# Scores behind the down projection, the last p*v ahead of it, and three edits that go with them, in a fused attention and gated-FFN kernel

## The chip, the core and the metric

One NeuronCore of a Trainium2 chip runs the whole program. Its engines are TensorE (PE: matmuls; PEld: the loads of their stationary operands), VectorE (DVE), ScalarE (ACT), GpSimd (POOL) and SyncE (SP, which here issues every DMA). The metric is the device time of one execution in microseconds, lower is better. Times in the text are microseconds unless marked otherwise.

## The reference

x has 2048 rows of D = 576. One branch is sliding-window attention with 32 heads of 18, the other a gated FFN of width 4608, and the two are multiplied.

```python
xn = _layernorm(x)
qkv = (xn @ wqkv) -> q, k, v, 32 heads of 18
scores = einsum("bhqd,bhkd->bhqk", q, k) * 18 ** -0.5
mask = (0 <= i - j) & (i - j < 256)
s = (softmax(where(mask, scores, -1e9)) @ v) @ wo
h = sigmoid(xn @ w_gate) * (xn @ w_up)
return x + s * silu(h @ w_down)
```

## The kernel before

**Chunks.** The rows are worked in four chunks of 512 (`NCH`, `CH`), each in four blocks of 128. A chunk has these stages on TensorE:

- *Projections* (L485): twelve passes, q, k and v of four blocks. For chunks 1 to 3 they stand between the down blocks 1 and 2 of the chunk before (`QKV_F2`). VectorE and ScalarE copy q and k out of PSUM, and transposing DMAs bring them into `qkp`.
- *Gate/up* (L873): 36 tiles of 128 columns of F, each with nine contraction steps. Two matmuls run at a time, one on rows 0 to 63 of the array (the low stream) and one on rows 64 to 127 (the high stream); a pair is called a step here. A tile's gate and up each take one of the banks 6, 7, 5, 4. ScalarE reads gate with a tanh (L887), VectorE combines it with up (L891) into `hT`. Since each stream does one of the two matrices, one gate tile, number `XS[c]`, has two of its steps moved to the high stream, ahead of its own turn, with weights loaded for it apart (`load_x`, L833); from there on gate ends two steps ahead of up.
- *Attention* between the gate/up steps: a score visit (L631) takes all of the banks 0 to 3 and feeds two exponentials on ScalarE (L649); VectorE applies the mask (L667). Chunks 1 to 3 have twenty such visits, chunk 0 sixteen. After each pair of head groups comes a p*v visit (L701), four in a chunk, also in banks 0 to 3, read out by VectorE transposes (L720, L722; in chunk 0 by L734, L736) and normalized; copies on SP (L228) collect the result in `oT`.
- *Down projection* (L1000): a block of 128 rows takes two banks, nine instructions of the planner with eight matmuls each (`f2`). ScalarE's tanh (L1062) and VectorE's L1064 read the block out of its banks. Chunk 0 does blocks 0 and 1 interleaved, all others go one by one. The last block of the kernel is split by columns (`build_last`, L1031).
- *Output projection* (L794, `wo`) in two pairs of blocks, after p*v's copies have landed. In chunks 0 to 2 it stands among the projections of the next chunk, in chunk 3 between down blocks 1 and 2.

**Tiling of the array.** The stages use TensorE differently: the down projection uses it whole ("full"), gate/up and the projections in two halves of 64 rows ("r64"), scores in four strips of rows ("r32"), p*v in four strips of columns ("c32").

**Order.** The program is built by a planner in the kernel itself. Each piece of work is an `Op` with an engine, a modelled duration, data dependences (`deps`, which become semaphore waits) and order-only dependences (`odeps`, which become none). `schedule` (L1074) places, over and over, the operation that can start first by its own model, with a small penalty for priority, and picks PSUM banks from the candidates of a `Psum`; `emit` (L1197) writes each engine's program in that order. So an order dependence changes what the planner does with everything after it.

**Around the change.** In `build_ffn`, `SC_GATE = 0` makes all score visits of chunks 1 to 3 wait, in order, for the chunk's first gate/up run (the test on `n0` at L975). The planner has put the first visit behind nine gate/up steps. `F2B` (L67) has the candidate banks of the last down block, `cands` (L987). Down block instructions other than block 0 have the last p*v of the chunk as an order dependence (L1007), which leaves the last p*v free to stand before or behind the last gate/up steps. In `build`, the weights of the output projection (`op_wo`, ten DMAs) become waits of the passes `wo:0:00` and `wo:0:10`.

Of the kernel before, what the change touches and what calls it, by code (L numbers as in the profile page):

```python
# [15 lines left out]
QPC = CH // P  # L16
NQB = S // P
NKT = 5
NHG = H // 4
# [4 lines left out]
NWD = NFT // WDG  # L24
# [23 lines left out]
RTH = 2  # L48
RREC = 2
RBN = 4  # L50
XS = (13, 1, 1, 1)
XP = (4, 0)
RUN = 3
WX_PRIO = -1
# [9 lines left out]
LAST = 448  # L64
W_GATE = 2
LAST_OUTS = 2
F2B = ((0, 1), (2, 3))  # L67
PVB = ((0,), (1,), (2,), (3,))

PRIO_NS = 40.0  # L70
# [39 lines left out]
def mm_ns(n):  # L110
    return max(28.0, n / 2.4 + 2.5)
# [76 lines left out]
class Builder:  # L188
# [99 lines left out]
    def build(self):  # L288
        self.r_xr = Ring(NXR)
        self.r_xnr = Ring(NXNR)  # L290
        self.r_xn = Ring(1)
        self.r_w = Ring(RW)
        self.r_t = Ring(RT)
        self.r_pk = Ring(RPK)
        self.r_exp = Ring(NEXP)
        self.r_s = Ring(RS)
        self.r_xf = Ring(RXF)
        self.r_th = Ring(RTH)
        self.r_rec = Ring(RREC)
        self.r_bn = Ring(RBN)  # L300
        self.op_f1 = {}
        self.build_init()
        self.op_pv = [[None] * NHG for _ in range(NCH)]
        self.op_sc = [[[] for _ in range(NHG)] for _ in range(NCH)]
        self.op_on = [[None] * NHG for _ in range(NCH)]
        self.op_oc = [[[], []] for _ in range(NCH)]
        self.op_v = [None] * NQB
        self.op_tail = [None] * NHG
        self.op_hT = {}
        self.f2_last = None  # L310
        for c in range(NCH):
            self.build_ln(c)
            if c == 0:
                self.build_weights()
                self.build_wd()
            self.build_qkv(c)
            self.last_mul = None
            self.build_attn(c)
            self.load_x(c)
            self.op_pkz = [self.op("POOL", 2000, lambda e: e.memset(self.pk[:, 1:RPK, :, :], 0.0), f"pkz:{c}",  # L320
                                   deps=self.op_on[c], prio=1)]
            if c == 0:
                self.op_wo = []
            self.build_wo(c)
            self.build_ffn(c)
            if c == 0:
                self.build_late_weights()
                for o in self.ops:
                    if o.name in ("wo:0:00", "wo:0:10"):
                        o.add_dep(self.op_wo)  # L330

    def build_init(self):
        op = self.op
# [491 lines left out]
    def load_x(self, c):  # L825
        self.sx, dx = self.r_s.take()
        f = XS[c] * P
        src = [(self.wg, f, 1, 64), (self.wu, (NFT - 1) * P, 0, 0)]
# [7 lines left out]
    def build_ffn(self, c):  # L836
        pg = [Psum((6,), (7,), (5,), (4,)) for _ in range(NFT)]
        pu = [Psum((6,), (7,), (5,), (4,)) for _ in range(NFT)]
        slots, dmas, sws = {}, {}, {}
        xs, xe = XS[c], NFT - 1  # L840
        gp = [i for i in range(NC) if LO[i] not in UP[0:2]]
# [22 lines left out]
        prev = None  # L864
        tile_end, tile_last = {}, {}

        def step(e, half, gu, ft, i, x):
            r0 = 64 * half
            f0 = ft % FG * P
            w = (slots[ft // FG][r0:r0 + 64, i, f0:f0 + P] if x is None  # L870
                 else self.sat[r0:r0 + 64, sx, x * P:(x + 1) * P])
            first, last = flags[(half, gu, ft, i)]
            return e.matmul(self.bank((pg, pu)[gu][ft]), w, self.xn[r0:r0 + 64, i, :], start=first, stop=last,  # L873
                            tile_position=(r0, 0))
# [29 lines left out]
        for n0, n1 in zip(cuts, cuts[1:]):  # L904
            deps, alloc, fence, done, ended = [prev], [], None, [], []
            for n in range(n0, n1):
                for half, st in enumerate((low, high)):
                    gu, ft, i, x = st[n]
                    fg = ft // FG
                    if x is None and fg not in slots:  # L910
                        far = c == 0 and fg == RW
                        sw, dw = (None, []) if far else self.r_w.take()
                        sws[fg] = sw
                        slots[fg] = self.far if far else self.wgs[:, sw, :, :]
                        wp = W_PRIO[fg] if c == 0 and fg <= RW else -2
                        fc = slice(fg * FG * P, (fg + 1) * FG * P)
                        ws = self.load9(slots[fg][0:64], slots[fg][64:P], self.wg[:, fc],
                                        self.wu[:, fc], f"w:{c}:{fg}", ("w", sw),
                                        dw + ([self.w_gate] if c > 0 and fg < RW else []), wp,
                                        W0_FACTOR if c == 0 and fg < 5 else 1.42)  # L920
                        dmas[fg] = ws
                        if c == 0 and fg == RW:
                            self.op_wx[1].add_dep(self.op_f1[(0, WX_FT)])
                        if c == 0 and fg in QKT_BEHIND:
                            for o in self.op_qkt[QKT_BEHIND[fg]:]:
                                o.behind = ws[-1:]
                    key = (gu, ft)
                    if key not in seen:
                        seen.add(key)
                        alloc.append((pg, pu)[gu][ft])  # L930
                        if self.f2_last and gu == 0:
                            deps.append(self.f2_last[ft // WDG])
                    if x is None:
                        deps.append(dmas[fg][(half if i < 5 - half else 2 + half)])
                        group_left[fg] -= 1
                        if group_left[fg] == 0:
                            ended.append(fg)
                    else:
                        deps.append(self.op_wx[gu])
                    if half != gu or key in ((0, xs), (1, xe)):  # L940
                        if tile_last.get(key, (half,))[0] != half:
                            fence = tile_last[key][1]
                    left[key] -= 1
                    if left[key] == 0:
                        done.append(key)
            if not prev:
                deps += self.all_xn

            def f(e, n0=n0, n1=n1):
                for n in range(n0, n1):  # L950
                    step(e, 0, *low[n])
                    r = step(e, 1, *high[n])
                return r
            o = self.pe((n1 - n0) * mm_ns(CH), f, f"f:{c}:{low[n0][1]}:{n0}", deps=deps, prio=3, psum=alloc, mode="r64")
            if fence:
                o.add_dep(fence)
                o.fence = fence
            for n in range(n0, n1):
                for half, st in enumerate((low, high)):
                    gu, ft = st[n][:2]  # L960
                    tile_last[(gu, ft)] = (half, o)
                    users = (pg, pu)[gu][ft].users
                    if users[-1] is not o:
                        users.append(o)
            for fg in ended:
                if sws[fg] is not None:
                    self.r_w.release(sws[fg], o)
            for key in done:
                tile_end[key] = o
                if key[0] == 0:  # L970
                    self.op_f1[(c, key[1])] = o
                if tile_end.get((1 - key[0], key[1])):
                    finish(key[1])
            prev = o
            if n0 == SC_GATE and c > 0:  # L975
                for l in self.op_sc[c]:
                    for u in l:
                        u.odeps.append(o)
        for o in self.op_se:
            o.add_dep(prev)  # L980
        mms = [prev]
        self.r_xn.release(0, prev)
        f2_last = [None] * NWD
        self.f2_ops = f2_ops = {}
        prev = mms
        for blocks in (((0, 1), (2,), (3,)) if c == 0 else ((0,), (1,), (2,), (3,))):
            cands = F2B if blocks[-1] == QPC - 1 else ((6, 7), (4, 5), (0, 1), (2, 3))  # L987
            banks = {i: Psum(*cands) for i in blocks}
# [3 lines left out]
            for q in range(NWD):  # L992
                for i in blocks:
                    def f_f2(e, q=q, i=i, ps=banks[i]):
                        b = ps.banks[0] * 512
                        for fl in range(WDG):
                            ft = q * WDG + fl
                            lhsT = self.hT[:, ft, i * P:(i + 1) * P]
                            for n0, n1 in ((0, 512), (512, D)):
# [4 lines left out]
                    o = self.op("PE", WDG * (mm_ns(512) + mm_ns(64)), f_f2, f"f2:{c * QPC + i}:{q}", deps, 3,  # L1004
                                alloc=[banks[i]] if q == 0 else [], mode="full",
                                odeps=prev + ([self.op_wop[i - RTH]] if q == 0 and i >= RTH else [])
                                + ([self.op_pv[c][NHG - 1]] if q == 0 and i > 0 else []))  # L1007
                    banks[i].users.append(o)
                    prev = [o]
# [306 lines left out]
```

## Time and profile before

| | us |
|---|---|
| median of 3 runs (lowest, highest) | 564.43 (564.29, 564.63) |
| the profiled execution, its own time | 564.39 |
| its span, first to last instruction | 562.2 |
| TensorE matmuls busy | 555.1 |
| VectorE busy | 305.4 |
| ScalarE busy | 279.1 |
| GpSimd busy | 29.3 |
| gate/up (L873, three groups) | 290.2 + 6.2 + 4.7 |
| down projection (L1000, L1031) | 131.1 + 9.0 |
| projections (L485) | 55.0 |
| scores (L631), p*v (L701) | 32.4, 20.7 |
| output projection (L794) | 18.8 |

The granted clock of TensorE is 1.000 over the span. A line of the profile names an engine, the line of the kernel, the operation, what it writes and reads, and the count. In a timeline the first two numbers are the start and the length of a merged group, and brackets at the end give the idle time before it and what ended that. Matmuls are pipelined and their ends are modelled, so lengths of neighbouring groups overlap; differences of starts do not have that fault. Some records of matmuls are missing (141 of 144 in a stretch of two down blocks), in the same places each time.

### The profile page before, as it was taken

The page shows a single profiled execution, that of the slowest core. Times are in us where ns is not written, and L with a number is a line of the kernel's source. Part 1 is how long each engine was busy: PE and PEld are TensorE (multiplying, and loading weights), DVE is VectorE, ACT ScalarE, POOL GpSimd, SP SyncE. Part 2 cuts the span into 40 slices and gives each one's busy share as a digit, 9 for nine tenths or more (in the row PEclk, how much of TensorE's full clock was granted, in tenths as well). Part 3 has the DMA queues.
Part 4 walks back from the last instruction along what each step waited for, and adds up shares of the span by engine and source line. Part 5 has one row for each costly group of instructions (what it writes and reads, how often), then busy time and mean ns, then how long its engine had stood idle before and what let it go on. Part 6 is the DMA issues. An engine that isn't in the chain of part 4 may idle for free.

```text
span 562.2 us, 17899 instructions
## 1 busy us (share of the span) xinstructions
PE 555.1 (99%) x7831; PEld 287.6 (51%) x7854; DVE 305.4 (54%) x656; ACT 279.1 (50%) x382; POOL 29.3 (5%) x55
## 2 busy tenths in 40 slices
PE   8999999999999999999999999999999999999997
PEld 5644444558544444456754444445665444444554
DVE  6135988722147886771215778766211586776312
ACT  7438877314065856811407576580230856856021
POOL 3000100100000110010000011001000000000100
PEclk9999999999999999999999999999999999999999
DMA  8999879839945766136793665604489355660010
GB/s 206 228 195 228 178 203 221 211 79 144 186 101 132 158 139 157 41 60 82 156 207 76 147 152 131 146 26 73 89 157 186 77 128 128 148 131 23 20 43 22
DMA packets 125898, 73.29 MB, mean 130 GB/s; under 512 B 54654, under 2 KB 125310, under 8 KB 125822
## 3 DMA queue, kind: packets, MB, share of 16 engines
q1 hardware_dynamic: 125822, 72.16, 61.1%
q8 instruction: 62, 1.02, 0.8%
q14 instruction: 14, 0.11, 0.1%
HBM read 55.48 MB, written 2.36 MB: 103 GB/s over the span
## 4 chain that ended last, share of the span: by engine, by line
PE 98%; DVE 1%; issue 0%; DMA 0%; ACT 0%
PE ps L873 51%; PE ps L1000 23%; PE ps L485 10%; PE ps L631 5%; PE ps L701 3%; PE ps L794 3%; PE ps L1031 2%; PE ps L461 0%; DMA xr<-in_A_x_dram 0%; DVE bnst L425 0%; DVE bnst L427 0%; DVE hT L891 0%; DVE op__63 L758 0%; DVE pk L722 0%; DVE mv L429 0%
## 5 line engine op out<-in xcount | busy, mean ns | idle before, releaser
L873 PE MATMUL ps<-xn,wgs 64*128 64x512 bf16 x2522 | 290.2, 377 | 0.0
L873 PEld LDWEIGHTS ps<-xn,wgs 64*128 64x128 bf16 x2522 | 116.2, 94 | 139.8 <-issue 10.0
L649 ACT ACTIVATE expr<-ps 128x1024 bf16<-128x1024 f32 x152 | 149.3, 1023 | 23.4 <-PE ps L631 23.4
L1000 PE MATMUL ps<-wd_sb,hT 128*128 128x64 bf16 (+1 forms) x1057 | 131.1, 284 | 2.1 <-issue 1.3
L891 DVE SCALAR_TENSOR_TENSOR hT<-tring,ps 128x512 bf16<-128x512 bf16 x144 | 98.1, 682 | 49.3 <-ACT tring L887 25.9
L887 ACT ACTIVATE tring<-ps 128x512 bf16<-128x512 f32 x144 | 86.3, 599 | 77.5 <-PE ps L873 58.3
L1000 PEld LDWEIGHTS ps<-wd_sb,hT 128*128 128x128 bf16 x1080 | 68.2, 98 | 65.0 <-issue 1.4
L1062 ACT ACTIVATE thf<-ps 128x576 bf16<-128x576 f32 (+2 forms) x17 | 10.6, 622 | 133.0 <-PE ps L1000 125.4
L667 DVE TENSOR_TENSOR expr<-expr,m 128x512 bf16<-128x512 bf16 (+2 forms) x152 | 58.1, 411 | 33.0 <-ACT expr L649 31.9
L1064 DVE SCALAR_TENSOR_TENSOR thf<-thf,ps 128x576 bf16<-128x576 bf16 (+2 forms) x17 | 12.2, 719 | 108.2 <-ACT thf L1062 108.1
L485 PE MATMUL ps<-wqkv_sb,xn 64*128 64x288 bf16 x864 | 55.0, 283 | 0.0
L485 PEld LDWEIGHTS ps<-wqkv_sb,xn 64*128 64x128 bf16 x864 | 42.8, 94 | 10.4 <-issue 0.5
L631 PEld LDWEIGHTS ps<-qkp 18*64 18x64 bf16 x1472 | 16.4, 103 | 32.9 <-ACT expr L649 19.1
L631 PE MATMUL ps<-qkp 18*64 18x320 bf16 (+4 forms) x1472 | 32.4, 259 | 0.1
L678 POOL COPY qkp<-qkp 128x256 bf16<-128x256 bf16 x24 | 9.9, 411 | 294.4 <-PE ps L631 294.4
L758 DVE STREAM_TRANSPOSE op__63<-pk 128x512 bf16<-128x512 bf16 x32 | 22.5, 702 | 0.2
L701 PEld LDWEIGHTS ps<-expr,vau 64*32 64x32 bf16 x1440 | 17.9, 92 | 7.2 <-issue 4.7
L701 PE MATMUL ps<-expr,vau 64*32 64x320 bf16 (+5 forms) x1440 | 20.7, 253 | 0.0
L1066 DVE TENSOR_TENSOR thf<-thf,sat 128x576 bf16<-128x576 bf16 (+2 forms) x17 | 7.5, 440 | 23.2 <-ACT sat L818 22.9
L794 PE MATMUL ps<-wo_sb,oT 64*128 64x288 bf16 x288 | 18.8, 283 | 0.2 <-issue 0.2
L540 ACT ACTIVATE pk<-ps 128x576 bf16<-128x576 f32 x13 | 8.5, 652 | 15.9 <-PE ps L485 13.6
L794 PEld LDWEIGHTS ps<-wo_sb,oT 64*128 64x128 bf16 x288 | 14.4, 94 | 3.6 <-issue 0.7
(62 smaller groups left out, 228.7 us busy)
## 6 DMA issues: line engine op xcount, KB each, us to landing
wgs<-in_B_w_gate_dram SPq DMA_DIRECT2D x47, 240.0 KB, 3.8
wgs<-in_B_w_up_dram SPq DMA_DIRECT2D x47, 240.0 KB, 4.8
wgs<-in_B_w_up_dram SPq DMA_DIRECT2D x47, 192.0 KB, 4.1
wgs<-in_B_w_gate_dram SPq DMA_DIRECT2D x47, 192.0 KB, 4.3
wd_sb<-in_B_w_down_dram SPq DMA_DIRECT2D x9, 576.0 KB, 6.5
xf<-in_A_x_dram SPq DMA_DIRECT2D x18, 144.0 KB, 2.7
out_dram<-xf SPq DMA_DIRECT2D x15, 144.0 KB, 2.0
xr<-in_A_x_dram SPq DMA_DIRECT2D x14, 144.0 KB, 4.4
```

Source lines behind the costliest of these rows:

```text
L485: r = e.matmul(self.bank(ps, HV, hf), self.xn[r0:r0 + 64, k, i * P:(i + 1) * P], self.wqkv_sb[r0:r0 + 64, j, k, :], start=(k == 0), stop=( ...
L631: r = e.matmul(self.ps[64 * half:64 * half + 64, b:b + n * 64], self.qkp[r0:r0 + DH, hg, k0:k0 + 64], self.qkp[r0:r0 + DH, hg, q0 * 64:(q0 ...
L649: return e.activation(self.expr[:, es, 2 * pr:2 * pr + 2, :], src, ACTF.Exp, scale=SM_SCALE)
L667: return e.tensor_tensor(ap, ap, m, ALU.mult)
L701: r = e.matmul(self.ps[32 * j:32 * j + 32, b + q0 * 64:b + (q0 + n) * 64], vf[:, v0:v0 + 32], self.expr[p0:p0 + 64, es, j, pos * 64:(pos + ...
L758: t2 = self.op("DVE", dve_ns(CH), lambda e, on=on: e.transpose(self.op_[:, hg % NOT, :], on.rearrange("p g d -> p (g d)")), f"t2:{c}:{hg}" ...
L794: r = e.matmul(self.bank(ps2[w], HV, n), self.oT[r0:r0 + 64, kt, qi * P:(qi + 1) * P], self.wo_sb[r0:r0 + 64, kt, n * HV:(n + 1) * HV], st ...
L873: return e.matmul(self.bank((pg, pu)[gu][ft]), w, self.xn[r0:r0 + 64, i, :], start=first, stop=last, tile_position=(r0, 0))
L887: return e.activation(self.tring[:, st_, :], self.bank(ps), ACTF.Tanh, scale=0.5)
L891: return e.scalar_tensor_tensor(self.hT[:, ft, :], self.tring[:, st_, :], 1.0, self.bank(ps), ALU.add, ALU.mult)
L1000: r = e.matmul(self.ps[:, b + n0:b + n1], lhsT, self.wd_sb[:, q, fl, n0:n1], start=(ft == 0), stop=(ft == NFT - 1))
L1064: q1 = self.rd("DVE", dve_ns(n), lambda e: e.scalar_tensor_tensor(t, t, 1.0, yap(), ALU.add, ALU.mult), f"fq1:{sb}:{c0}", deps=[th], prio= ...
```

## The change

Five edits:

1. The first score visit of chunks 1 to 3 is put, by order, behind the last instruction of the down projection before it, and the chunk's first gate/up run behind that visit. The other visits keep their dependence on the first gate/up run.
2. The last down block of chunks 0 to 2 takes its banks from 6, 7 or 4, 5 in place of 0, 1 or 2, 3.
3. The gate tile with the two moved steps is number 2 in place of number 1 in chunks 1 to 3.
4. The last p*v of every chunk gets the last gate/up run as an order dependence, and the down projection gets that p*v in place of the gate/up run.
5. The ten loads of the output projection's weights become waits of the nine instructions of chunk 0's down block 1 too (the tenth goes to the first again).

```diff
-XS = (13, 1, 1, 1)
+XS = (13, 2, 2, 2)
...
-F2B = ((0, 1), (2, 3))
+F2B = ((6, 7), (4, 5))
...
                 for o in self.ops:
                     if o.name in ("wo:0:00", "wo:0:10"):
                         o.add_dep(self.op_wo)
+                for k, o in enumerate(self.op_wo):
+                    self.f2_ops[(1, k % NWD)].add_dep(o)
...
             if n0 == SC_GATE and c > 0:
+                first = min((u for l in self.op_sc[c] for u in l), key=lambda u: u.cidx)
                 for l in self.op_sc[c]:
                     for u in l:
-                        u.odeps.append(o)
+                        if u is not first:
+                            u.odeps.append(o)
+                first.odeps.append(self.f2_ops[(QPC - 1, NWD - 1)])
+                o.odeps += [first] if n0 == 0 else []
         for o in self.op_se:
             o.add_dep(prev)
         mms = [prev]
+        self.op_pv[c][NHG - 1].odeps.append(prev)
+        mms = [self.op_pv[c][NHG - 1]]
         self.r_xn.release(0, prev)
```

## The prediction

> **What bounds the kernel now.** Read first the page's busy line and its chain of work.
>
> ```profile
> PE 555.1 (99%) x7831; PEld 287.6 (51%) x7854; DVE 305.4 (54%) x656; ACT 279.1 (50%) x382; POOL 29.3 (5%) x55
> PE 98%; DVE 1%; issue 0%; DMA 0%; ACT 0%
> ```
>
> TensorE is busy for 99% of the span and is 98% of the chain, so the time is TensorE's stream of instructions laid end to end. The edits add and remove no matmul; they can only change what is lost where the stream passes from one kind of work to another, or where it waits. Those places I read in the timeline of TensorE. Ends of matmuls are modelled there, so I use starts alone.
>
> ```profile
> 197.59 7.29 PE L873 MATMUL ps<-xn,wgs 64*128 64x512 bf16 x66
> 204.81 0.42 PE L631 MATMUL ps<-qkp 18*64 18x320 bf16 x16
> 205.17 2.76 PE L873 MATMUL ps<-xn,wgs 64*128 64x512 bf16 x24
> ...
> 208.22 2.55 PE L873 MATMUL ps<-xn,wgs 64*128 64x512 bf16 x22
> 210.70 0.42 PE L631 MATMUL ps<-qkp 18*64 18x256 bf16 x16
> ```
>
> Two matmuls are one gate/up step, one on each half of the rows. From the first start of a gate/up stretch to the visit behind it, 33 steps take 204.81 - 197.59 = 7.22 us and 11 steps 2.48. One step is (7.22 - 2.48)/22 = 0.2155, and 2.48 - 11 x 0.2155 = 0.11 is what each stretch loses at its end. A score visit (L631) takes 205.17 - 204.81 = 0.36. **So a stretch that is joined to its neighbour saves 0.11 us.** The other stretches fit this within 0.02, but for the eight named under the rivals.
>
> **First score visit, chunks 1 to 3.** Chunk 1 now:
>
> ```profile
> 140.00 17.59 PE L1000 MATMUL ps<-wd_sb,hT 128*128 128x64 bf16 x141 [0.16 <-issue]
> 157.52 1.25 PE L873 MATMUL ps<-xn,wgs 64*128 64x512 bf16 x9
> ...
> 159.57 0.42 PE L631 MATMUL ps<-qkp 18*64 18x320 bf16 x16
> 159.93 2.33 PE L873 MATMUL ps<-xn,wgs 64*128 64x512 bf16 x20
> ```
>
> Down projection, 9 steps of gate/up (2.05), scores. Afterwards: down projection, scores, gate/up without that break. One stretch end goes, 0.11, if the down projection hands over to scores at the cost at which it hands over to gate/up. That handover is not in the trace. The nearest rows: two down blocks take 17.52 from their first start to the next work's, whether that is gate/up (157.52 - 140.00), the projections (260.14 - 242.62) or the output projection (536.74 - 519.22); and gate/up loses the same 0.11 before p*v (14 steps, 512.10 to 515.23: 3.13). So the loss does not depend on what comes next, and I take it as equal. On the dear side stands the passage from projections to down projection: 108 matmuls take 6.95 (133.05 to 140.00) where 72 take 4.42 (260.14 to 264.56), so 6.95 - 1.5 x 4.42 = 0.32 too much; a handover dearer by that would turn -0.11 into +0.21. On the cheap side it could save its own loss too, another 0.1. Sum: 3 x -0.11 = **-0.33**, bounds -0.63 and +0.63.
>
> The Trainium skill, "TensorEngine Tiling (Array Packing)", Key Properties, says that a change of tiling mode drains TensorE; the 0.11 agrees in kind. "TensorE: Matmul & The Clock Gate", Single matmul latency, has 166 ns as the constant part of a lone warm matmul; as an estimate from that page, the five changes saved here and below would be 0.83 in place of my 0.53.
>
> The scores need the query and key transposes; chunk 1's last is issued at 139.8, and the slowest of all took 8.0 to land: 147.8 at worst, before 157.5. The visit's waits now stand behind the down projection instead of behind gate/up, with longer matmuls to cover them. POOL's copies behind the scores (L678) come earlier on an engine that is 5% busy.
>
> **Last down block in gate/up banks.** Scores need banks 0 to 3 at once, so block 3 goes to two of the banks 4 to 7; gate/up's first tile takes the other two, and its second tile, nine steps later, needs block 3's. When are they read out? ScalarE, then VectorE, in chunk 1:
>
> ```profile
> 157.69 0.65 ACT L1062 ACTIVATE thf<-ps 128x576 bf16<-128x576 f32 x1 [8.17 <-PE ps L1000]
> ...
> 160.18 1.94 ACT L649 ACTIVATE expr<-ps 128x1024 bf16<-128x1024 f32 x2
> ```
>
> ```profile
> 158.37 0.76 DVE L1064 SCALAR_TENSOR_TENSOR thf<-thf,ps 128x576 bf16<-128x576 bf16 x1 [7.01 <-ACT thf L1062]
> ```
>
> The reads end at 158.37 + 0.76 = 159.13. The second tile would start at 157.52 + 0.36 + 9 x 0.2155 = 159.82: 0.7 of slack, cost nothing. The cover is that the tanh (L1062) goes ahead of the exponentials of the first scores; the planner orders ScalarE by readiness, and the tanh is ready as the block ends, the exponentials 0.4 later. XS = 2 moves the early bank of a gate tile to step 13, at 160.7; ScalarE is then through that tanh, two exponentials and the first gate tanh, 157.69 + 0.6 + 1.8 + 0.6 = 160.7: just in time, and the second score visit, ready by 160.2, can go between. Taken as nothing, bounds 0 and 0.3 a chunk. The early weights (L833) are loaded as before, 25 us ahead.
>
> **Last p*v ahead of the down projection.** Chunks 1 and 2 have this order already (241.10 below), so chunks 0 and 3 change.
>
> ```profile
> 101.94 1.11 PE L701 MATMUL ps<-expr,vau 64*32 64x320 bf16 x72
> 102.98 1.04 PE L873 MATMUL ps<-xn,wgs 64*128 64x512 bf16 x8
> 104.18 17.59 PE L1000 MATMUL ps<-wd_sb,hT 128*128 128x64 bf16 x141 [0.16 <-issue]
> ```
>
> ```profile
> 241.10 1.35 PE L701 MATMUL ps<-expr,vau 64*32 64x320 bf16 x96
> 242.62 17.59 PE L1000 MATMUL ps<-wd_sb,hT 128*128 128x64 bf16 x141 [0.16 <-issue]
> ```
>
> From p*v to gate/up it is 1.28 in chunk 3 (515.23 to 516.51), from p*v to the down projection 1.52: 0.24 more. Chunk 0 now: 1.04, then 1.20 for four steps and the entry. Then: four steps joined to the stretch before, 0.86, and 1.04 + 0.24: 2.14 against 2.24. Chunk 3 now: 1.28 + 2.71 (11 steps, 516.51 to 519.22); then 11 x 0.2155 + 1.52 = 3.89 against 3.99. Together **-0.20**, from rows, within 0.05.
>
> What moves with it: p*v's VectorE chain and its eight copies into oT, later by 0.9 in chunk 0 and 2.4 in chunk 3. In chunk 3 SP issues them from 522.16 for 6.05, and they land 1.8 later, near 530; the output projection starts at 536.74, so 4 are left. In chunk 0 they go out from 109.94 to 115.43, held back by transposes of the next rows ahead of them in SP's queue; behind them stand four more transposes, out by 120.6, which the first projection at 121.70 does not wait for; the output projection comes at 126.44. No cost; without that slack up to 0.9 and 2.4. Chunk 0 also starts two down blocks one microsecond apart; the second needs the last gate/up tile's banks, read out 1.7 after its end now (VectorE's L891 ends at 105.72) and needed 1.28 + 1.0 = 2.3 after it: hidden.
>
> **Waits of wo spread.** Chunk 0's first output pass waits for ten weight loads besides sixteen copies and two bank releases; chunk 1's for the other eighteen alone.
>
> ```profile
> 121.70 4.58 PE L485 MATMUL ps<-wqkv_sb,xn 64*128 64x288 bf16 x72
> 126.44 2.38 PE L794 MATMUL ps<-wo_sb,oT 64*128 64x288 bf16 x36 [0.15 <-issue]
> ```
>
> ```profile
> 260.14 4.58 PE L485 MATMUL ps<-wqkv_sb,xn 64*128 64x288 bf16 x72
> 264.56 2.37 PE L794 MATMUL ps<-wo_sb,oT 64*128 64x288 bf16 x36
> ```
>
> 4.74 against 4.42: **-0.32**. The row blames "issue": the loads were in. The waits move to the nine instructions of down block 1, whose neighbours of block 0 each wait for a w_down load already: that stretch is 104.18 to 121.70 = 17.52, and 17.52 in chunk 1 without such waits. They cost nothing there if the loads have landed; the last is issued at 95.0, the slowest of the ten took 9.9, and block 1 starts near 105.2. Bounds -0.32 and 0.
>
> **Sum.** -0.33 - 0.20 - 0.32 = -0.85. The profiled execution took 564.39 (span 562.2), 0.04 under the median of the three runs: 563.54, so **563.5 us**, -0.15%. A measurement of this kernel tells some 0.2% (1.13 us) from no change, so this counts as the same.
>
> **Rivals.**
> - *Other waits go.* The chain has one stall: at 342.99 scores wait 0.21 for VectorE's transposes of p*v; and seven score visits start 0.06 late, behind exponentials. All visits now come nine steps earlier against gate/up's tiles. For: such waits hang on where VectorE's row statistics fall. Against: the same shift can make new ones. If they go: 563.54 - 0.21 - 0.42 = 562.9. Chance 0.18.
> - *A saved change is worth more than 0.11*, as much as the entry to the full array costs above the return to gate/up (0.24): 5 x 0.24 + 0.32 = 1.52, 562.9. Against it, chunks 1 and 2 show the price of the p*v order directly. 0.05. The skill's drain rule above points this way.
> - *The handover to scores is dear*: 564.39 + 0.63 - 0.52 = 564.5; no row speaks for it. 0.08.
> - *Block 3's banks come free late.* If both exponentials go ahead of the tanh, the reads end 0.4 + 1.8 later, at 161.3, and the second tile starts 1.5 late in three chunks: 563.54 + 4.5 = 568.0, **slower**. It costs from the point where the reads end over 2.3 after the down projection (now 1.6). For: both are ready within half a microsecond; against: the order of readiness. 0.08.
> - The forecast: 0.61.
>
> The range holds the forecast and the first three rivals, not the fourth: 562.9 to 564.5. Faster by over 0.2% (under 563.30): the first two rivals and a tenth of the forecast, 0.29. Slower 0.08. Same 0.63.
>
> **What would show it.** Right: scores (L631) start 17.52 behind the first of the last two down blocks, with no gate/up between; L701 to L1000 takes 1.28 in chunk 0 and 1.52 in chunk 3; the first L794 comes 4.42 behind L485. Wrong: a gap at the second gate/up tile, ended by L1064 or L1062; over 17.7 from L1000 to L631; a gap inside chunk 0's first down stretch, ended by a DMA.

## The result, and the profile after

| | before | changed |
|---|---|---|
| median (lowest, highest), same chip | 564.43 (564.24, 565.02), 11 runs | 568.57 (566.36, 573.41), 11 runs |
| ratio of the times, 95% interval | | 1.0073 (1.0053 to 1.0092) |
| the profiled execution, its span | 564.39, 562.2 | 568.60, 566.4 |

The changed kernel is slower by 0.7%, 4.1 us; the forecast was 563.5, in a range of 562.9 to 564.5. The scatter has grown too: 7 us between lowest and highest, where the kernel before has 0.8.

The page of the changed kernel: busy line, granted clock, the two DMA queues that matter here, and the chain.

```profile
PE 558.5 (99%) x7854; PEld 286.5 (51%) x7854; DVE 306.4 (54%) x656; ACT 279.2 (49%) x382; POOL 28.9 (5%) x55
...
PEclk9999999999999999999999999999999989999999
...
q1 hardware_dynamic: 125822, 72.16, 60.9%
q8 instruction: 62, 1.02, 0.8%
...
PE 98%; DVE 1%; issue 1%; DMA 0%; ACT 0%
```

Two things are new: one slice of the clock row is 8, and the chain has 1% of "issue", time in which TensorE waited for nothing that the profile shows. The q8 line stood on the page before as well, with the same 62 transfers, and I had passed over it.

The chain of the changed kernel puts the "issue" at one place, in chunk 3 behind the first p*v stretch; then the timeline of TensorE around it.

```profile
449.12 1.28 PE ps L703 x89
450.40 0.54 PE ps L875 x4
450.94 3.15 issue
454.08 5.99 PE ps L875 x40
```

```profile
445.13 0.43 PE L633 MATMUL ps<-qkp 18*64 18x320 bf16 x24
445.49 3.63 PE L875 MATMUL ps<-xn,wgs 64*128 64x512 bf16 x32
449.05 1.35 PE L703 MATMUL ps<-expr,vau 64*32 64x320 bf16 x96
450.33 0.61 PE L875 MATMUL ps<-xn,wgs 64*128 64x512 bf16 x4
454.08 5.99 PE L875 MATMUL ps<-xn,wgs 64*128 64x512 bf16 x40 [3.15 <-issue]
460.00 0.42 PE L633 MATMUL ps<-qkp 18*64 18x320 bf16 x16
```

22 gate/up steps go from 450.33 to 460.00 = 9.67. By the prediction's own figures they take 22 x 0.2155 + 0.11 = 4.85. **So 4.8 us are lost in this one stretch.** The instruction at 454.08 waits on no semaphore; there simply is nothing executed between 450.94 and 454.08. The rest is the clock; windows of the changed kernel (columns: window, its length, busy time and count by engine, granted clock, DMA share, GB/s):

```profile
450.94:454.08 3.14, 0.00 (x0) 0.00 (x0) 0.96 (x2) 0.00 (x0) 0.00 (x0) 0.95 0.89 184
454.08:457.10 3.02, 3.02 (x16) 1.08 (x18) 1.70 (x3) 0.00 (x0) 0.00 (x0) 0.50 0.05 12
457.10:460.00 2.90, 2.90 (x29) 1.16 (x25) 1.76 (x5) 1.19 (x2) 0.00 (x0) 0.99 0.00 0
```

For 3 us behind the idle stretch the clock is 0.50, and seven steps take twice their time: 7 x 0.2155 = 1.5 lost. With the 3.15 idle and 0.16 for the last pair ahead of it (450.56 to 450.94, in place of 0.2155) this makes the 4.8. 568.60 - 4.82 = 563.78 is the profiled execution without the stall. (Its first projection, ahead of every edit, starts 0.25 later than in the profile before, 7.48 against 7.24, so the order itself gains some 0.85 there and not 0.6.)

**What TensorE waits for is its own program.** The q8 line is the supply: 62 transfers of 16 KB for the 15,945 instructions that TensorE records (7,854 matmuls, as many weight loads, and 237 waits and drains), one for each 256. I read them out of the trace's DMA records and set them beside the count of executed instructions, with matmuls whose record is missing counted in. Numbered from 0, transfer k brings the block whose first instruction is number 256k + 449: all the gaps that are told below stand there. Around the stall:

```
            starts   ends     instruction 256k+448   instruction 256k+449
before 49   448.52   449.46   executed at 452.48     executed at 452.48
after  49   451.20   452.48   executed at 450.56     executed at 454.08
after  50   455.21   456.49   executed at 465.85     executed at 465.92
```

The stream stops exactly at the first instruction of block 49, and goes on 1.6 us after that block has landed. In the kernel before the same block has landed 3.0 us ahead of its use.

How much time there is for a refill can be counted too. Over the sixteen profiles of the experiments below and the two of before and after, no transfer from block 10 on starts more than 293 instructions ahead of its block, and half of them start less than 238 ahead. Gate/up executes 4 instructions in 0.2155 us, so 293 are 15.8 us; but a p*v stretch is 192 instructions in 1.28 us, and a score visit 32 to 48 in 0.36. Block 49's 293 instructions hold a visit of 24 matmuls, or most of it, and a p*v stretch. They last 6.1 us in the kernel before (446.38 to 452.48) and some 5.8 (445.17 to 450.94) in the changed one.

The Trainium skill, "Runtime: NRT & Kernel Launch", Instruction fetch mechanics, describes this: a sequencer drives its own DMA queue and fetches its program in blocks of 16 KiB, 256 instructions. The trace agrees with the block and the queue (62 x 16 KB on q8). The same section calls the cost "mostly hidden" and gives TensorE room for 2048 instructions; here it runs dry 293 instructions behind the earliest start of a transfer, and the cost is 4.8 us.

### The profile page after: what moved, and what is told of

The parts are those of the page before. It is cut to its first block, busy times and chain, and to the rows that moved or that the text cites. A ratio compares the mean times of both kernels' runs of the same rounds, so it can differ in the third digit from the quotient of the medians.

```text
span 566.4 us, 17915 instructions
## 1 busy us (share of the span) xinstructions
PE 558.5 (99%) x7854; PEld 286.5 (51%) x7854; DVE 306.4 (54%) x656; ACT 279.2 (49%) x382; POOL 28.9 (5%) x55
## 4 chain that ended last, share of the span: by engine, by line
PE 98%; DVE 1%; issue 1%; DMA 0%; ACT 0%
PE ps L875 51%; PE ps L1008 24%; PE ps L487 9%; PE ps L633 5%; PE ps L703 3%; PE ps L796 3%; PE ps L1039 2%; PE ps L463 0%; DMA xr<-in_A_x_dram 0%; DVE bnst L427 0%; DVE bnst L429 0%; DVE mv L431 0%; DVE xnr L440 0%; DVE thf L1072 0%; ACT thf L1070 0%
## 5 line engine op out<-in xcount | busy, mean ns | idle before, releaser
L1008 PE MATMUL ps<-wd_sb,hT 128*128 128x512 bf16 (+1 forms) x1080 | 133.7, 286 | 0.0
L320 POOL MEMSET pk<- 128x2048 bf16 x4 | 7.2, 1804 | 176.5 <-DVE op__63 L760 176.5
```

Source lines behind the costliest of these rows:

```text
L1008: r = e.matmul(self.ps[:, b + n0:b + n1], lhsT, self.wd_sb[:, q, fl, n0:n1], start=(ft == 0), stop=(ft == NFT - 1))
```

## The experiments

Theory A: the reordering did what the prediction said, and the loss is TensorE running out of instructions, because the edits moved where the refills fall. Rival B: the new order itself costs the time. Later rivals concern why the refill is late. "Before" is the kernel before on the same chip as each group of experiments: medians 564.74, 564.61, 564.62 and 564.58 (lowest 564.21, highest 565.25).

Most experiments move the refills without moving any work. A down matmul over 576 columns is made as two, of 512 and of 64; in the first `PAD` of them in chunk 0 that can be cut, the 512 are cut into two of 256. So `PAD` weight loads and `PAD` matmuls more stand ahead of chunk 1; the arithmetic is the same.

```diff
-                            for n0, n1 in ((0, 512), (512, D)):
+                            cut = c == 0 and 0 < ft < 35 and i * 34 + ft <= PAD
+                            for n0, n1 in ((0, 256), (256, 512), (512, D)) if cut else ((0, 512), (512, D)):
```

**e1: the changed kernel once more.**

> The changed kernel once more, for a second profile. In its first profile TensorE stands still for 3.15 us from 450.94, in the middle of a gate/up stretch of chunk 3, at an instruction that waits for no semaphore; the profile calls it issue. Theory A (instruction refill): TensorE's program comes in 62 blocks of 16 KB by DMA (queue 8), and block 49 starts only at 451.20, behind a burst of gate/up weight loads, when all loaded instructions are used up. Then the stall is at the same instruction again, 1 to 8 us long, with a late queue-8 transfer beside it, and nowhere else; the rest of the stream takes 563.5. Theory B (a data wait that the profile does not name, on weights or banks): the stall is at that place too, but its end has nothing to do with queue 8. Theory C (chance, a disturbed execution): the stall is elsewhere or absent and the time 563.5.

570.0 (one execution). Two stalls this time:

```profile
332.08 1.35 PE L703 MATMUL ps<-expr,vau 64*32 64x320 bf16 x96
333.37 0.39 PE L875 MATMUL ps<-xn,wgs 64*128 64x512 bf16 x2
336.72 7.08 PE L875 MATMUL ps<-xn,wgs 64*128 64x512 bf16 x64 [2.96 <-issue]
343.73 0.42 PE L633 MATMUL ps<-qkp 18*64 18x320 bf16 x16
```

This one is block 36 in chunk 2, whose transfer started at 333.93 (330.72 in the first profile, in time), the other block 49 again. A third, of 0.3 us, is at block 52. So lateness varies from one execution to the next at the same instruction, which fits the scatter. Behind 2.96 us of idle time the clock stays at full speed (64 matmuls in 7.08), behind 3.15 it did not.

**e2 and e3: 16 and 64 cuts, the changed order untouched.**

> The changed kernel with 16 of the 512-column matmuls of chunk 0's down block 0 cut into two of 256: 32 instructions more ahead of everything that follows (a load and a matmul each), some 0.05 us of work more, no wait, bank, load or order changed. It shifts where the 16 KB blocks of TensorE's program (256 instructions each) end, by 32 instructions or 1.7 us of gate/up. Theory A: block 49 is asked for earlier than in the changed kernel, the p*v visit that eats 192 instructions in 1.3 us comes 32 instructions later against the block's end, as in the kernel before, and the stall goes: 563.5 to 563.7. Theory B: the stall stays, 566 to 573.

564.58 (563.57 to 565.60, ten runs), ratio 0.9996 (0.9986 to 1.0007). Half of the executions lie at 563.6 to 563.9, the others at 565.3 to 565.6; the profiled one, 563.61, has no stall. **32 instructions more, with all the work in the same order, take 4 us off.**

> The same with 64 matmuls cut (blocks 0 and 1 of chunk 0): 128 instructions, half a block of program, 0.2 us of work more. Theory A: block ends fall elsewhere, no stall at 450; 563.6 to 563.9 unless another block comes late (the shortest time to use up a block's lead is then near 488). Theory B: the stall stays at 450, 566 to 573.

566.10 (565.91 to 568.16), ratio 1.0030 (1.0018 to 1.0043). Blocks 36 and 49 are in time, but block 18 starts 2.2 us into chunk 1's first p*v stretch and its first instruction comes at 177.64, 1.4 behind its landing. The stall has moved, as A has it.

**e4: the second of the two weight bursts around the stall issued later.**

```diff
-                                        dw + ([self.w_gate] if c > 0 and fg < RW else []), wp,
+                                        dw + ([self.w_gate] if c > 0 and fg < RW else [])
+                                        + ([self.op_f1[(c, 7)]] if c == NCH - 1 and fg == 4 else []), wp,
```

> The changed kernel with one dependence more: the weight loads of gate/up group 4 in chunk 3, issued at 448.07 to 450.65 now, also wait for gate tile 7, some 3.5 us later. TensorE's program is the same instruction for instruction. Theory A: block 49 finds the DMA queues empty after 447 and comes before the burst; no stall at 450; 563.5 to 564. If the block is late whatever the loads do, the stall stays. Theory B with weights: a later load makes the stall longer or leaves it.

565.55 (563.68 to 568.28), ratio 1.0013 (0.9999 to 1.0027). Block 49 still starts late, at 450.50, though the last weight load ahead of it had landed at 448.86 and the next was issued at 454.62. The idle stretch shrinks to 0.95. So the weight loads make it worse, as far as one profile and the ten times tell, but aren't all of it.

**e5 and e11: the kernel before, its order untouched, with 108 and 46 cuts.**

> The kernel before, unchanged but for 108 of chunk 0's 512-column down matmuls, each cut into two of 256 columns: 216 more TensorE instructions ahead of chunk 1, and nothing moved. This puts the 50th refill's request some 95 instructions ahead of chunk 3's p*v stretch, where it stands in the changed kernel, instead of 136. Theory A (the stall belongs to where the instruction refills fall): the unchanged kernel now runs dry too, near p*v of chunk 2 or 3, with an idle stretch of 1 to 4 us and, behind a long one, matmuls at half rate: 566 to 570. Rival B (the stall belongs to the changed order of the work): no idle stretch, 564.2 to 564.8 (16 and 64 such cuts moved chunk 0's down projection by -0.2 and -0.1 us).

565.41 (565.22 to 565.84), ratio 1.0015 (1.0006 to 1.0024). The forecast of A, 566 to 570, failed: block 50 started 2.7 us ahead of p*v, in time. The offset (by how much the same work comes later than in the trace of before) grows by 0.26 over the cut down blocks, the cuts' own cost, and by 0.2 and 0.3 behind p*v stretches of chunks 2 and 3, at the first instructions of blocks 40 and 53, each 1.4 behind its landing.

> The kernel before, nothing moved, with 46 of chunk 0's 512-column down matmuls cut in two: 92 more TensorE instructions ahead of chunk 1. Its first p*v stretch of chunk 1 then begins 39 instructions behind the point at which the block's room comes free, as in the run with 64 cuts (38), which lost 1.8 us there. Theory A (the loss comes from where the refills fall, whatever the order): TensorE runs dry behind chunk 1's first p*v stretch (near 175 us) by about 1 to 2.5 us, 565.5 to 567. Rival B (it needs the changed order): no idle stretch, 564.5 to 564.9 with the cuts' own cost of 0.1 to 0.2 us.

565.02 (564.47 to 566.12), ratio 1.0008 (0.9999 to 1.0018), no stall in the profiled one (564.47): block 18, at the same distance from p*v as in e3, started 2.9 us ahead of the stretch, there 2.2 behind its beginning. **So the distance alone doesn't decide**, and the long stall was not reproduced in the unchanged order; only the short one was.

**e6: a fifth of the weight bytes.**

```diff
+            if small:
+                dst, src = dst[:, 0:1, :], src[:, 0:1, :]
...
```

> The changed kernel with the same instructions on every engine, but in chunks 1 to 3 each weight load from group 3 on moves only one of its four or five row blocks, a fifth to a quarter of the bytes and packets (the gate and up products of those groups use old weights in the rest, so that part of the computation is left out). Theory A1 (the refill is late because the weight loads keep the DMA engines busy): every refill starts within about 2 us of its request, no idle stretch of TensorE in chunks 1 to 3, 563.6 to 564.0. Rival A2 (the refill is late for a reason in TensorE's own sequencer, such as the dense p*v stretch): the idle stretch near p*v of chunk 3 stays, 566 to 570.

565.42 (564.86 to 569.16), ratio 1.0027 (1.0014 to 1.0041). Both theories were half wrong: the stall is there, but half as long.

```profile
448.85 1.35 PE L705 MATMUL ps<-expr,vau 64*32 64x320 bf16 x96
450.13 0.61 PE L877 MATMUL ps<-xn,wgs 64*128 64x512 bf16 x4
452.25 4.49 PE L877 MATMUL ps<-xn,wgs 64*128 64x512 bf16 x40 [1.50 <-issue]
```

Block 49 starts 1.0 us after the p*v stretch began (2.15 in the changed kernel) and takes 0.93 (1.28). In this profile the bytes are worth some 1.5 us of the 3; the rest has another cause. The loads themselves are still issued, as many as before.

**e13: most of that p*v stretch left out.**

```diff
-                for m in range(max(len(side) for side in runs[hg])):
+                short = c == NCH - 1 and a == 0
+                for m in range(1 if short else max(len(side) for side in runs[hg])):
...
```

> The changed kernel with chunk 3's first p*v stretch cut from 96 matmuls to 16 (the rest of that part of p*v is left out). Everything up to its first instruction is the changed kernel. Theory P (the dense stretch holds the refill of block 49 back): the transfer starts within some 0.5 us of the end of the short stretch, near 449.8 or earlier instead of 451.2 on the time line of the changed kernel, 1.7 to 2.2 us earlier than there. Theory Q (the request is late before the stretch begins): it starts at the same distance from the beginning of p*v as before, +0.4 to +2.2 us. In both the block that is being executed lasts longer, since 160 instructions are gone from it, so no idle stretch there; 563.2 to 563.8 unless another block runs dry.

564.32 (563.03 to 566.38, eight runs). Block 49 starts at 454.19 on this time line, 2.1 behind the beginning of p*v at 452.10, as in the changed kernel (2.15). Theory Q: the length of the dense stretch doesn't hold the transfer back. Nothing stalls there, since the stretch now leaves time enough. (The profiled execution, 565.94, has the 3 us stall at block 36 as e1 had.)

**e7, e12, e14, e15, e16: other cuts in the changed order.**

> The changed kernel with 24 of chunk 0's 512-column down matmuls cut in two: 48 more TensorE instructions ahead of chunk 1. Theory A: the 300 instructions behind the request of block 49 now last 6.8 instead of 5.8 us, and those of block 36 7.2 instead of 5.6, so both get through; the shortest that is left is block 52's, 6.3. If it holds too, the time is that of the changed kernel without the stall, 563.5 to 563.8, below the kernel before; if block 52 runs dry now and then, single executions are 1 to 5 us longer. Rival B (the stall belongs to the changed order): 566 to 570 as in the changed kernel.

566.19 (563.57 to 568.17, twelve runs), ratio 1.0019 (1.0001 to 1.0038): five executions at 563.6 to 564.0, the others at 566.1 to 568.2. The profiled one, 563.66, has no stall; A's time came in five of twelve, and no trace shows what the other seven lost.

> The changed kernel with 32 of chunk 0's 512-column down matmuls cut in two: 64 more TensorE instructions ahead of chunk 1. The p*v stretches of chunks 2 and 3 then begin 68 to 178 instructions behind the point at which a block's room comes free, but for the last two, 16 and 44 (the changed kernel: 36 to 111, and 4 and 56 in chunk 3). Theory A: starts of refills 1 to 5 us ahead of those stretches, so no idle stretch up to 490 us; the last two decide: 563.5 to 563.8 in executions without one there, some 0.5 to 3 us more in those with one. Rival B (the changed order costs the time): 566 to 570.

564.31 (564.14 to 565.15), ratio 0.9998 (0.9989 to 1.0006). One stall of 0.45 is left, at block 55, in the stretch that had been named as doubtful.

> The changed kernel with 2 of chunk 0's 512-column down matmuls cut in two: 4 more TensorE instructions. Chunk 3's first p*v stretch then begins 60 instead of 56 instructions behind the point where the block's room comes free. If lateness is a matter of a few instructions around one event (another kernel had its transfer in time at 59): the stall behind that stretch goes in most executions, 563.6 to 565.5. If lateness grows smoothly with the distance: still 566 to 570.

567.38 (564.28 to 569.47), ratio 1.0044 (1.0018 to 1.0070). In the profiled execution (564.32) block 49 starts 2.3 us ahead of p*v; three of eight executions take 564.3 to 564.7 like that one, the others 3 to 5 us more. Neither form of the expectation: chances change over a few instructions, not the length of the stall.

> As e14, with 6 cut matmuls, 12 more instructions: chunk 3's first p*v stretch begins 68 instructions behind, chunk 2's second and third 71. If a few instructions decide: no stall there, 563.6 to 564.5. If smooth: about the same loss as in the changed kernel or slightly less, 565 to 568.

564.78 (563.59 to 571.10), ratio 1.0031 (1.0000 to 1.0061): seven executions at 563.6 to 565.4, three at 569.7 to 571.1. The profiled one stalls at blocks 49 and 52, by 0.4 and 0.7.

> The changed kernel with 44 cut matmuls, 88 more instructions. The distances of the p*v stretches of chunks 1 to 3 are then 254, 202, 202, 179; 199, 147, 147, 124; 144, 92, 40, 68. Only the third of chunk 3 is in the doubtful stretch of 28 to 60, where 12 of the 23 profiled ones so far started in time with room to spare. Theory A: 563.6 to 564.0 in executions without a stall, faster than the kernel before by 0.6 to 1.0 us; 564.5 to 566 in those in which that one is late.

564.03 (563.89 to 564.28, eleven runs), ratio 0.9991 (0.9982 to 1.0000). (The count of 12 in 23 in the expectation was not taken from the traces. Counted over all of them, 44 p*v stretches begin 28 to 60 instructions behind the point that lies 256 instructions ahead of a block, which is what the expectations call its room coming free, and 36 of their transfers started ahead of the stretch.) The two places that stalled in the changed kernel and in e12, now whole:

```profile
449.29 1.35 PE L704 MATMUL ps<-expr,vau 64*32 64x320 bf16 x96
450.57 4.92 PE L876 MATMUL ps<-xn,wgs 64*128 64x512 bf16 x44
455.43 0.42 PE L634 MATMUL ps<-qkp 18*64 18x320 bf16 x16
```

```profile
491.78 1.35 PE L704 MATMUL ps<-expr,vau 64*32 64x320 bf16 x96
493.07 4.92 PE L876 MATMUL ps<-xn,wgs 64*128 64x512 bf16 x44
```

22 steps take 4.86 at the first, there is no idle time at either, nothing runs dry in the profiled execution, and the scatter is down to 0.4 us. **The changed order measures 0.55 us less than the kernel before where its instructions arrive in time.** That is half of what a measurement of this kernel tells from no change, and the interval reaches 1.0000; the highest of its eleven runs lies below the median of before.

**e8, e9, e10: parts alone.** Sizes are read from the offset of each stage's end against the trace of before.

> Only the fifth edit: the waits on wo's loads spread over the second down block of chunk 0. The prediction's term for it is -0.32 us (32 TensorE waits ahead of the first output projection, of which 0.32 us stood open). If that holds and no refill of instructions falls badly: 564.1. If the waits cost as much in the down block: 564.4. If the waits that leave shift the instruction blocks into a bad place: an idle stretch that the trace shows, 565 or more.

564.81 (564.49 to 565.64), ratio 1.0006 (0.9997 to 1.0014). The output projection comes early by the forecast amount:

```profile
121.85 4.58 PE L487 MATMUL ps<-wqkv_sb,xn 64*128 64x288 bf16 x72
126.28 2.37 PE L796 MATMUL ps<-wo_sb,oT 64*128 64x288 bf16 x36
```

126.28 - 121.85 = 4.43. The offset falls by 0.32 there and grows by some 0.3 at the first instruction of block 39, 1.6 behind its landing. A gain given back at a refill, in a kernel that moves no work at all.

> Only the first three edits: the first score visit of chunks 1 to 3 behind the down projection, gate and up run 0 joined to the next, block 3 in the gate and up banks. The prediction's terms for them are 3 x -0.11 = -0.33 us. Theory A: the offset against the trace of before changes by -0.11 behind each first score visit, nothing is lost at block 3's banks, and whatever the total shows beyond -0.33 is an idle stretch that starts exactly at the first instruction of a refilled block and ends 1.3 to 1.6 us behind that refill's transfer: 564.2 without one, up to 568 with one. Rival B (the joined stretch or the borrowed banks themselves cost time): the loss stands at the score visits or at the next chunk's gate and up tiles, and no refill is near.

564.74 (564.38 to 565.10), ratio 1.0002 (0.9993 to 1.0011). Chunk 3 gains 0.11 as forecast. Chunk 1 gains nothing, and chunk 2 only the 0.21 of the wait at 342.99, which block 39 takes back (0.27). Also, the wait of the first output pass is 0.15 shorter here than in the profile of before, with the same waits; e5, e10 and e11 show the same 0.15.

> Only the fourth edit: the last p*v stretch of chunks 0 to 3 directly ahead of the down projection. The prediction's term is -0.20 us, from chunks 0 and 3. Theory A: 564.4 without an idle stretch, more with one at the first instruction of a refilled block. Rival B: a loss at the down projection's first matmuls, which would wait for p*v.

564.37 (564.18 to 564.90), ratio 0.9999 (0.9989 to 1.0008). Chunk 0 gains 0.11 as forecast, chunk 3 nothing.

## Why the prediction was wrong

**The step that failed** is the first one: the edits "can only change what is lost where the stream passes from one kind of work to another, or where it waits". There is a third way to lose time, the supply of the instructions themselves, and no rival named it. The page's q8 line was the way to it: 62 refills, and stages in which 192 instructions go by in 1.28 us. Seventeen gaps of 0.27 to 3.5 us from one instruction's start to the next's, in the profiles of the changed kernel and the experiments, stand exactly at the first instruction of a block, and each ends 1.35 to 1.63 us after that block's transfer. The kernel before has none; its tightest block is used 2.0 us after landing.

Shown: the time is lost to late refills (each of those gaps); it hangs on where they fall and not on the order as such (e2, e16: the same order, up to 4.5 us less; e8: a loss with no work moved); the weight loads make it worse (e4, e6). Not shown: why a transfer that starts in nearly four cases of five within 100 instructions of its earliest point is sometimes 293 late. It isn't the p*v stretch (e13), not the distance to it alone (e3 against e11), and not the traffic alone (e6). **That stays open.** Since the unchanged order with 46 and 108 cuts lost at most 0.5 us in its profiles, the changed order may also be more prone to it; two counts can't tell.

The traces narrow it, though no run was made to test this. Of 937 refills from block 10 on, half start within 1.7 us of their earliest point (293 instructions ahead), and one in twenty later than 4.6. The five that left TensorE idle for 1.8 us or more (e1 twice, e3, e13, the changed kernel) took 5.2 to 6.0, and in each of them SyncE issued four weight loads meanwhile. The transfer starts 0.1 to 0.6 behind the last issue, block 49 of e13 too (0.5); in the changed kernel it does so at 451.20:

```profile
448.07 0.59 SPq L228 DMA_DIRECT2D wgs<-in_B_w_gate_dram  x1
448.71 0.62 SPq L228 DMA_DIRECT2D wgs<-in_B_w_up_dram  x1
449.38 0.62 SPq L228 DMA_DIRECT2D wgs<-in_B_w_gate_dram  x1
450.03 0.62 SPq L228 DMA_DIRECT2D wgs<-in_B_w_up_dram  x1
```

Over the 463 such bursts of all profiles, 10 refills start in the 1.5 us up to 0.5 ahead of a burst's end, and 107 in the 1.5 us after that; in e6, with small loads, 1 and 9. So what goes with the late starts is the issuing of the loads more than their bytes. It isn't all: in e4 block 49 had no such burst beside it and still took 4.3.

**The sum, point by point**, from the offsets of the changed kernel against the trace of before:

| step | forecast | measured |
|---|---|---|
| chunk 1 (first score visit) | -0.11 | 0.00 |
| chunk 2 (without the wait at 342.99) | -0.11 | +0.01 |
| chunk 3 | -0.11 | -0.11 |
| last p*v, chunks 0 and 3 | -0.20 | -0.11, -0.10 |
| waits of wo | -0.32 | -0.32 |
| the wait at 342.99 (a rival) | 0 | -0.21 |
| sum | -0.85 | -0.84 |

The sum held, but partly by luck: two losses of 0.11 that had no price, in chunks 1 and 2, are made up by a wait that had been put among the rivals. (That 568.6 lies near the 568.0 of the rival about block 3's banks is chance too.) *First score visit:* the handover costs what was assumed; in the changed kernel's timeline:

```profile
139.59 17.81 PE L1008 MATMUL ps<-wd_sb,hT 128*128 128x512 bf16 x144
157.33 0.42 PE L633 MATMUL ps<-qkp 18*64 18x320 bf16 x16
157.69 2.55 PE L875 MATMUL ps<-xn,wgs 64*128 64x512 bf16 x22
```

157.33 - 139.59 = 17.74 with all 144 records there. Before, the first of the 144 is missing (and two further on): the weight loads begin at 139.77, the recorded matmuls at 140.00, and the stretch seemed 0.22 shorter.

```profile
139.77 0.36 PEld L1000 LDWEIGHTS ps<-wd_sb,hT 128*128 128x128 bf16 x4 [0.24 <-issue]
```

So the "over 17.7" that was to show a dear handover is met by the records alone. The same missing record made the passage from p*v to the down projection seem 0.24 dearer, and most of the 0.32 between projections and down projection; with the record there p*v to down is 242.21 - 240.93 = 1.28 in chunk 1, as from p*v to gate/up, and 108 matmuls take 6.71 (132.88 to 139.59) against 1.5 x 4.42 = 6.63. The rival that rested on the 0.24 had nothing under it; in the term for p*v the 0.24 stood on both sides and fell out. Within the sum, what failed is the joined stretch at the end of chunks 1 and 2. Weight loads of TensorE, then VectorE, in chunk 1 of the changed kernel:

```profile
238.34 0.09 PEld L875 LDWEIGHTS ps<-xn,wgs 64*128 64x128 bf16 x1
238.88 1.19 PEld L875 LDWEIGHTS ps<-xn,wgs 64*128 64x128 bf16 x14 [0.44 <-DVE hT L893]
```

```profile
237.46 0.76 DVE L669 TENSOR_TENSOR expr<-expr,m 128x512 bf16<-128x512 bf16 x2 [1.53 <-ACT expr L651]
238.14 0.68 DVE L893 SCALAR_TENSOR_TENSOR hT<-tring,ps 128x512 bf16<-128x512 bf16 x1
```

The up tile's bank comes free when VectorE's product ends at 238.14 + 0.68 = 238.82, and the product stands behind two masks of a score visit that now comes nine steps earlier. The next weight load is at 238.88, 0.54 behind the last where two steps are 0.43: 0.11 lost, at 377.00 in chunk 2 again, and at 515.77 in e10. The prediction had said that the shift "can make new" waits, and had given them no price.

*Last p*v:* right in the changed kernel. In e10, without the other edits, chunk 3 loses its 0.11 to the same bank.

*Waits of wo:* right against the profiled execution, but four other profiles of the old waits lose 0.17 there and not 0.32, so the edit is worth some 0.17 in a usual execution, and the whole change some 0.7. e16, with about 0.1 of cost for its cuts, measures 0.55.

*Block 3's banks:* no wait there in any of the three chunks, as forecast.

## What to carry to other kernels

Where an engine is busy for 99% of the span, its own instruction stream is a resource: read the instruction queue's line on the page, and ask in which 300 instructions the least time passes. A reorder, a dropped wait or one more instruction moves every later refill, so compare versions by the places of their stalls before judging an order by its time, and look at the scatter: 7 us in place of 0.8 was the sign. A few added instructions ahead of the tight place can settle it, for the price of those instructions and only for this one program.

## What the runs showed that was not expected

- TensorE's program comes in 62 transfers of 16 KB (61 to 63 in the experiments), 0.9 to 1.8 us each, and an instruction of a new block is executed no sooner than 1.35 us after its transfer ends.
- A transfer starts at the earliest 293 instructions ahead of its block; in the worst cases (e1, e13, the changed kernel) it starts only when the block before is used up.
- Idle stretches of 2.87 to 2.96 us left the clock at full speed; in one of 3.15 it was halved. In the changed kernel's trace the low clock lasts 3.41 us:

```profile
453.74:457.15 3.41, 3.07 (x16) 1.14 (x18) 1.70 (x3) 0.00 (x0) 0.00 (x0) 0.50 0.06 13
```

The Trainium skill, "TensorE: Matmul & The Clock Gate", Part 1, puts the window at about 3.4 us; the low stretch agrees. That the clock fell at 453.74, 2.80 behind the modelled end of the last matmul, is less than such a window of idle time, but as the ends are modelled the trace doesn't settle how long TensorE must be idle.
